# Chunked attention and two feed-forward layers on one core: a fourth attention tile in the banks of h, a fixed line of first loads, the sign of the weights moved from ScalarE to VectorE

## The chip, the cores and the metric

The kernel runs on one core of one Trainium2 chip. The metric is the device time of one execution in microseconds (us); several runs are timed and their median is taken. TensorE (PE) does matmuls and transposes, VectorE (DVE) and ScalarE (ACT) work element by element and read the matmul results out of PSUM, GpSimd (POOL) works on SBUF, and the queue of SyncE (SP) issues every DMA of this kernel. Each engine takes its instructions in the order of its queue.

## The reference, cut to what matters

```
# attention within chunks of 64 tokens; 4 batches, 8 heads, 576 tokens, head size 64
scores = scale * (q_c @ k_c.T);  scores -= scores.max(-1)
attn = exp(scores);  attn = attn / (attn.sum(-1) + 1e-09)
x = (attn @ v_c)                         # as 2304 tokens x 512
h = x @ w_in1;   g = max(h, 0) + log1p(exp(-abs(h)));   x = g @ w_out1
h = x @ w_in2;   g = P(h) / (Q(h) + 1e-6);              out = g @ w_out2
```

Inputs arrive as 8-byte floats; w_in is 512 x 2048 and w_out 2048 x 512 in both layers. P is a cubic and Q a quadratic in |h| with four and two given coefficients.

## The kernel before

**Tiling.** Attention works on 18 tiles of 128 tokens. The layers work on five blocks of tokens, BLOCKS (L25): 512, 512, 512, 384 and 384, in the order 0, 3, 4, 1, 2 (L26, L27). A block passes through 16 steps, one for each slice of 128 hidden units: a step is twelve matmuls into h (`products_h`, L750), the activation on ACT, DVE and POOL (`softplus`, L787, or `rational`, L812), and twelve matmuls (nine or twelve in layer 2) into acc. A product of two 4-byte floats is made of three matmuls: each operand is split into a rounded high part and a low part, the rest (`split`, L282). ACT or POOL writes the high part, DVE or POOL the low part.

**Weights.** A weight chunk is loaded as 8-byte words and put together in `prepare` and `complete`: ACT makes a magnitude out of the upper words (`magnitude`, L338), DVE shifts it (`shift`, L351) and ORs in three bits of the lower words (`merge`, L357). Where a chunk is signed, ACT keeps the sign with a Prelu, which needs the table set EXP_LN loaded; where it is not, the magnitude is a Copy, which asks for no set, and DVE merges the sign with a second `merge`. Then the chunk is split: the high part of w_in on ACT, that of w_out on POOL (L389), both low parts on DVE. SIGNED (L36) covers the sixteen steps of block 0, in which all chunks of layer 1 are converted, two to a step. The softplus of those steps needs ACT's other set, so `table` (L254) loads a set each time the two alternate.

**Start.** Block 0 needs attention tiles 0 to 3 (STARTING) before its first product, h_0. A tile is: transposes of q and k on PE (L512), taken to SBUF by ACT (L524, into `room` for the first four tiles), scores (L558), maximum, subtraction, exponential, total, guard, reciprocal and division (L576 to L611, ACT only for the exponential), a transpose of the result (`turn_e`, L618), taken by ACT (L640), times v (`values`, L647), and split into xT (L290 on ACT, L298 on DVE). The tiles need two PSUM banks each: tiles 0 and 3 take the pair of pool ps_att, one after the other, tiles 1 and 2 the two pairs of ps_acc. The two banks of ps_h hold h; the first is used ahead of that by `warm`, matmuls of an identity with itself (`keep_warm`, L1150) that fill the time in which the plan has PE idle before h_0. Tiles 12, 13 and 14 follow within block 0; the others are done beside blocks 3, 4 and 1, with q and k and the result turned on DVE.

**Order.** All work is put down as tasks with an engine, a cost in us and what they depend on (`Program.add`, L68). `schedule` (L168) lists them several times, backwards for due times and forwards, first by the earliest due time, and keeps the list that ends soonest by these costs; the instructions are then emitted in that order of time. So a change of one cost or one dependence can move instructions on every queue. `alloc` ties tasks that take buffers of one pool into the order in which the buffers turn.

Of the kernel before, what the change touches and what calls it, by code (L numbers as in the profile page):

```python
# [11 lines left out]
F32 = mybir.dt.float32  # L12
# [23 lines left out]
SIGNED = range(0, 16)  # L36
# [3 lines left out]
E_BY_VECTOR = {*range(4, 12), *range(15, 18)}  # L40


class Program:
# [49 lines left out]

    def run(self, links, counts, place, free, pick, place_of):
# [34 lines left out]
    def forward(self, place):  # L129
        loaded = [None]  # L130
# [59 lines left out]
def tile_chunk_attention_two_ffn(  # L190
# [91 lines left out]
    def split(dst, src, hi_eng, lo_eng, cost, reads, key, alloc=None, before=None):  # L282
# [20 lines left out]
        add(lo_eng, lo_cost, lo, [*reads, (key, 0)], [(key, 1)])  # L303
# [17 lines left out]
    def prepare(name, after, signed):  # L321
# [47 lines left out]
        add(DMA, 2.2, load, [], [rkey], alloc="raw", after=after)  # L369
# [5 lines left out]
    def complete(name, rkey, mkey, shift, merge, signed):  # L375
# [5 lines left out]
        if layer == 1 or fc in DIRECT:  # L381
            key = wkey[name] = turn("w" + which, FC)

            def alloc():
# [4 lines left out]
                lambda n: wts[name][:, n], lambda: x["m", name], ACT if which == "i" else POOL,  # L389
# [39 lines left out]

    xT = {}  # L430
# [4 lines left out]
    unfinished = []  # L435
# [8 lines left out]
    def attention(tb):  # L444
# [3 lines left out]
        by_chunk = tb in E_BY_VECTOR  # L448
        o0 = 4 * CH if by_chunk else 0
# [70 lines left out]
        def take(n):  # L520
            def f():
                if n == 0:
                    new_turned()
                act.activation(  # L524
                    tiles["qkT"][:, n].rearrange("p g t -> p (g t)"), ps[0][:, n], AF.Copy
# [20 lines left out]
        def scores():  # L546
# [3 lines left out]
            for g in range(4):  # L550
                for c in range(2):
                    for h in range(2):
                        part_h, chunk = slice(64 * h, 64 * h + 64), slice(c * CH, (c + 1) * CH)
                        o0 = (2 * g + c) * CH
                        o = ps[0][part_h, 0, o0 : o0 + CH]
# [13 lines left out]
        def sc():  # L569
            if by_chunk:  # L570
                return ps[0][:, :, : 4 * CH].rearrange("p h (g k) -> p h g k", k=CH)
            return ps[0][:, 0].rearrange("p (m k) -> p m k", k=CH)
# [37 lines left out]
        def divide():  # L610
            vec.tensor_tensor(  # L611
# [4 lines left out]
        def turn_e():  # L616
            for g in range(4):
                pe.transpose(  # L618
                    ps[0][:, 0, g * P : (g + 1) * P],
# [18 lines left out]
        def take_e():  # L638
            tiles["aT"] = new_e(1)
            act.activation(tiles["aT"].rearrange("p m k -> p (m k)"), ps[0][:, 0], AF.Copy)  # L640

        def values():
            for g in range(4):
                for c in range(2):
                    for h in range(2):
                        part_c = slice(c * CH, (c + 1) * CH)
                        pe.matmul(  # L647
                            ps[0][64 * h : 64 * h + 64, c, o0 + g * CH : o0 + (g + 1) * CH],
# [10 lines left out]
        def half(n):  # L659
            tile = xT[1, j][:, n, :, part * TB : (part + 1) * TB]  # L660
            return tile.rearrange("p g (c t) -> p g c t", c=2)

        def result():
# [38 lines left out]
        if not by_chunk:  # L702
            add(DMA, 1.46, load_v, [], [(vkey, 0)])
# [14 lines left out]
        add(DVE, 0.6, divide, [ke, ks], [ke])  # L718
# [478 lines left out]
```

## Time and profile before

| | |
|---|---|
| median of 3 runs | 859.34 us (859.08 to 859.9) |
| the profiled execution's own time | 860.32 us |
| its span, first to last instruction | 858.5 us |
| granted clock of TensorE, mean | 0.999 |
| busy: PE, DVE, ACT, POOL | 99%, 75%, 59%, 30% of the span |
| ACT_TABLE_LOAD | 35 of 1.283 us, 31 of them between 31.4 and 127.4 us |
| first matmul of h_0 | 31.46 us |
| first matmul of block 3 (end of block 0's steps) | 127.38 us |

The profile lists the instructions of one execution with start and duration. Busy time says how much of a stretch an engine worked; the chain of waits and the idle time before an instruction say what it waited for. The profiled execution lies 1.0 us above the median, and 1.8 us of its time lie outside its span.

### The profile page before, as it was taken

What the parts mean: (1) busy time and instruction counts of PE and PEld (TensorE: products, weight loads), DVE (VectorE), ACT (ScalarE), POOL (GpSimd) and SP (SyncE); (2) the same over time, 40 slices, a digit from 0 to 9 for tenths busy, and PEclk for the clock granted to TensorE, in tenths of its full rate; (3) what the DMA queues carried; (4) which work ended last, traced back from release to release, by engine and by line L of the source; (5) the groups of instructions that cost most, each with busy time, mean ns of one, the idle gap of its engine ahead of it and who ended that gap; (6) DMA issues with size and microseconds to landing.
All of it is one profiled execution on the core that took longest, in us unless ns stands there. A gap on an engine that the chain in (4) does not pass through costs nothing.

```text
span 858.5 us, 13274 instructions
## 1 busy us (share of the span) xinstructions
PE 846.5 (99%) x5070; PEld 729.4 (85%) x5070; DVE 646.6 (75%) x1102; ACT 505.7 (59%) x862; POOL 258.3 (30%) x238
## 2 busy tenths in 40 slices
PE   8999999999999999999999999999999999999997
PEld 8777889999999888888778888899889888888886
DVE  3877788798899987217956687878787787788684
ACT  4899983323335323344447675768667776667683
POOL 0132432122321222143363622342252162222121
PEclk9999999999999999999999999999999999999999
DMA  9874535112552443246532200100200020000001
GB/s 204 210 224 149 192 104 124 38 50 84 167 144 74 147 111 100 74 136 205 172 101 90 84 0 1 50 1 1 75 12 1 7 80 0 1 14 36 0 1 49
DMA packets 76927, 71.11 MB, mean 83 GB/s; under 512 B 36160, under 2 KB 63808, under 8 KB 76864
## 3 DMA queue, kind: packets, MB, share of 16 engines
q1 hardware_dynamic: 76864, 70.27, 28.4%
q8 instruction: 39, 0.64, 0.3%
q14 instruction: 24, 0.20, 0.1%
HBM read 56.63 MB, written 13.63 MB: 82 GB/s over the span
## 4 chain that ended last, share of the span: by engine, by line
PE 79%; DVE 13%; issue 3%; ACT 3%; DMA 1%; POOL 0%; SPq 0%; DVEq 0%; ACTq 0%; POOLq 0%
PE h L759 38%; PE acc L951 22%; PE acc L921 16%; DVE qkT L537 4%; DVE aT L631 2%; DVE cm_2o L362 1%; PE aps L558 1%; DVE cm_2i L362 1%; PE warm L1153 1%; DVE t L832 1%; PE aps L647 1%; DMA wr_2o<-in_moe_w_out_dram 1%; PE aps L512 1%; DVE sm L601 1%; DVE mx L576 0%
## 5 line engine op out<-in xcount | busy, mean ns | idle before, releaser
L921 PE MATMUL acc<-g,w_1o 128*128 128x512 f32 (+1 forms) x960 | 211.7, 369 | 0.0
L759 PE MATMUL h<-xT,w_1i 128*128 128x512 f32 (+1 forms) x960 | 210.2, 369 | 1.5 <-ACT g L799 1.3
L759 PE MATMUL h<-xT,w_2i 128*128 128x512 f32 (+1 forms) x960 | 209.3, 368 | 0.4 <-DVE t L832 0.4
L951 PE MATMUL acc<-w_2o,g 128*128 128x512 f32 x864 | 208.9, 391 | 0.6 <-DVE ev L986 0.5
L759 PEld LDWEIGHTS h<-xT,w_2i 128*128 128x128 f32 x960 | 175.8, 188 | 26.0 <-DVE t L832 1.4
L759 PEld LDWEIGHTS h<-xT,w_1i 128*128 128x128 f32 x960 | 174.1, 188 | 25.3 <-ACT g L799 2.7
L921 PEld LDWEIGHTS acc<-g,w_1o 128*128 128x128 f32 x960 | 174.1, 188 | 23.0 <-DVE ev L986 0.2
L951 PEld LDWEIGHTS acc<-w_2o,g 128*128 128x128 f32 x864 | 161.3, 188 | 34.8 <-POOL g L862 1.8
L862 POOL TENSOR_TENSOR g<-t,g 128x512 fp32r<-128x512 f32 (+1 forms) x80 | 94.6, 1182 | 263.1 <-ACT g L859 221.9
L802 POOL TENSOR_TENSOR g<-t,g 128x512 fp32r<-128x512 f32 (+1 forms) x80 | 99.9, 1248 | 223.3 <-ACT g L799 209.6
L794 ACT ACTIVATE t<-h 128x512 f32<-128x512 f32 (+1 forms) x80 | 44.2, 552 | 93.8 <-PE h L759 93.7
L799 ACT ACTIVATE g<-h 128x512 fp32r<-128x512 f32 (+1 forms) x80 | 44.3, 554 | 65.4 <-PE acc L921 59.9
L537 DVE STREAM_TRANSPOSE qkT<-qk 32x256 f32<-32x256 f32 x176 | 76.8, 437 | 5.7 <-PE aps L558 2.4
L832 DVE SCALAR_TENSOR_TENSOR t<-u,absb_t,t 128x512 f32<-128x512 f32 (+1 forms) x80 | 55.4, 694 | 30.5 <-ACT u L829 17.4
L888 DVE TENSOR_TENSOR t<-h,t 128x512 f32<-128x512 f32 (+1 forms) x80 | 50.8, 635 | 34.6 <-ACT t L847 21.0
L851 ACT ACTIVATE u<-t,epsq_t 128x512 f32<-128x512 f32 (+1 forms) x80 | 52.0, 650 | 37.5 <-DVE t L832 35.5
L832 DVE SCALAR_TENSOR_TENSOR t<-t,epsq_t,u 128x512 f32<-128x512 f32 (+1 forms) x80 | 55.4, 692 | 20.5 <-ACT u L855 20.1
L859 ACT ACTIVATE g<-t 128x512 fp32r<-128x512 f32 (+1 forms) x80 | 46.8, 586 | 37.0 <-DVE t L832 36.7
L832 DVE SCALAR_TENSOR_TENSOR t<-t,na_t,h 128x512 f32<-128x512 f32 (+1 forms) x80 | 55.4, 693 | 10.9 <-ACT t L847 7.0
L847 ACT ACTIVATE t<-h,b_t 128x512 f32<-128x512 f32 (+1 forms) x80 | 51.0, 640 | 18.0 <-PE h L759 10.4
L877 ACT ACTIVATE t<-h,na_t 128x512 f32<-128x512 f32 (+1 forms) x80 | 58.4, 730 | 4.5 <-PE h L759 4.5
L832 DVE SCALAR_TENSOR_TENSOR u<-t,na_t,u 128x512 f32<-128x512 f32 (+1 forms) x80 | 55.7, 697 | 0.0
(79 smaller groups left out, 751.6 us busy)
## 6 DMA issues: line engine op xcount, KB each, us to landing
wr_1i<-in_moe_w_in_dram SPq DMA_DIRECT2D x16, 512.0 KB, 3.8
wr_1o<-in_moe_w_out_dram SPq DMA_DIRECT2D x16, 512.0 KB, 4.5
wr_2i<-in_moe_w_in_dram SPq DMA_DIRECT2D x16, 512.0 KB, 4.0
wr_2o<-in_moe_w_out_dram SPq DMA_DIRECT2D x16, 512.0 KB, 3.8
out_dram<-ev SPq DMA_DIRECT2D x18, 256.0 KB, 2.1
qk<-in_q_dram SPq DMA_DIRECT2D x16, 256.0 KB, 5.3
qk<-in_k_dram SPq DMA_DIRECT2D x16, 256.0 KB, 5.9
v<-in_v_dram SPq DMA_DIRECT2D x16, 256.0 KB, 4.6
```

The lines of the kernel that those rows point to most:

```text
L537: vec.transpose(tiles["qkT"][p0 : p0 + 32, n, :, c * CH : (c + 1) * CH].rearrange("p g (u t) -> p g t u", t=2), qk_t[tb][p1 : p1 + 32, h:: ...
L759: pe.matmul(hs[s], w[:, a, c * P : (c + 1) * P], xt[:, b, c, :n_tok], start=n == 0, stop=n == 3 * KC - 1,)
L802: pool.tensor_tensor(out=gs[s][:, 1, :n_tok], in0=t["t2"], in1=gs[s][:, 0, :n_tok].bitcast(F32), op=ALU.subtract,)
L832: return lambda: vec.scalar_tensor_tensor(out=out(), in0=in0(), scalar=scalar, in1=in1(), op0=op0, op1=op1)
L847: act.activation(new("t1"), h(), AF.Abs, scale=b_t[:, 0:1])
L851: act.activation(u(), d(), AF.Ln, bias=epsq_t)
L859: act.activation(gs[s][:, 0, :n_tok], p(), AF.Copy)
L862: pool.tensor_tensor(out=gs[s][:, 1, :n_tok], in0=p(), in1=gs[s][:, 0, :n_tok].bitcast(F32), op=ALU.subtract,)
L877: lambda: act.activation(new("t2"), h(), AF.Identity, scale=na_t[:, 3:4], bias=na_t[:, 2:3]),
L888: lambda: vec.tensor_tensor(out=p(), in0=h(), in1=p(), op=ALU.mult), [hkey, kp], [kp],
L921: pe.matmul(accs[1, j, half][:, c % 2, :n_tok], wts[1, "o", fc][:, a, c * P : (c + 1) * P], gs[s][:, b, :n_tok], start=first and n == 0, s ...
L951: pe.matmul(accs[2, j, half][:, c % 2], gs[s][:, b, c * P : (c + 1) * P], wts[2, "o", fc][:, a, :], start=first and n == 0, stop=last and ...
```

## The change

Five things are changed.

1. **Tile 3 in the banks of h** (`apart`): the fourth tile takes the two banks of ps_h as two tiles of one bank each, instead of the pair of ps_att after tile 0. Its result is split bank by bank, in two halves on ACT and on DVE. `warm` gives its bank up when tile 3 takes its own, and from then on nothing fills PE's idle time until tile 0's low part of xT is done; after that `warm_2` takes the pair of ps_att.
2. **First loads in a fixed line** (`in_line`, FIRST_LOADS): sixteen loads are tied in the order q and k of the four tiles, v of tiles 0 and 1, w_in chunk 0, v of 2 and 3, w_in chunk 1, w_out chunk 0, q of tile 12. A second line puts tile 12's transposes behind tile 3's result.
3. **Sign of the weights**: SIGNED is now range(2), so the chunks put down in steps 0 and 1 (w_in 0 to 2, w_out 0 and 1) stay as they were, and of the other 27 chunks DVE merges the sign with an instruction of its own. The magnitudes of these no longer ask for EXP_LN.
4. **Rounding**: ACT, not POOL, writes the high part of the w_out chunks of layer 1 that are not signed.
5. **Costs in the plan**: loads of q, k and v 1.2 us (were 1.45 and 1.46), of weights 1.5 us (were 2.2), and the plan starts with EXP_LN loaded. DIVIDE_BY_POOL is empty and so does nothing.

```
-SIGNED = range(0, 16)
+SIGNED = range(2)
+FIRST_LOADS = "q0 k0 q1 k1 q2 k2 q3 k3 v0 v1 i0 v2 v3 i1 o0 q12".split()
...
+    def in_line(self, tasks):
+        for a, b in zip(tasks, tasks[1:]):
+            self.deps[b].setdefault(a, 0.0)
...
-        add(DMA, 2.2, load, [], [rkey], alloc="raw", after=after)
+        loads[which, fc, layer] = add(DMA, 1.5, load, [], [rkey], alloc="raw", after=after)
...
-                lambda n: wts[name][:, n], lambda: x["m", name], ACT if which == "i" else POOL,
+                lambda n: wts[name][:, n], lambda: x["m", name], ACT if which == "i" or (layer == 1 and not signed) else POOL,
...
+        apart = tb == STARTING[-1]
...
+        def bank(n):
+            return ps[n] if apart else ps[0][:, n]
+
         def new_ps():
+            if tb not in STARTING[:-1]:
+                x["warm"] = None
+            if apart:
+                for n in range(2):
+                    ps[n] = ps_h.tile([P, 512], F32, tag="h", name=f"aps_{tb}_{n}")
+                return
...
+        def result(c=None):
+            if apart:
+                return ps[c][:, : 4 * CH].rearrange("p (g t) -> p g t", t=CH)
...
+        if apart:
+            alloc = "h"
...
-        b0, b1 = (slot, 0), (slot, 1)
+        b0, b1 = (turn("h", 2), turn("h", 2)) if apart else ((slot, 0), (slot, 1))
...
-            split(half, result, ACT, DVE, 512, [b0, b1], (xkey[1, j], part), "x", new_x)
+            if not apart:
+                done[tb] = split(
+                    half, result, ACT, DVE, 512, [b0, b1], (xkey[1, j], part), "x", new_x
+                )
+                return
+            for c, b in ((0, b0), (1, b1)):
+                done[tb] = split(
+                    lambda n, c=c: half(n, c), lambda c=c: result(c), ACT, DVE, 256, [b],
+                    (xkey[1, j], (part, c)), "x", new_x,
+                )
...
+    prog.in_line(
+        [loads[(l[0], int(l[1:]), 1) if l[0] in "io" else (l[0], int(l[1:]))] for l in FIRST_LOADS]
+    )
+    prog.in_line([done[STARTING[-1]], begin[STAGED[len(STARTING)], 0]])
...
-            for _ in range(int(time / 0.22)):
+            for _ in range(int(time / 0.22) if x["warm"] else 0):
                 pe.matmul(x["warm"][:, :P], ident, ident, start=True, stop=True)
...
+            if i == done[STARTING[0]]:
+                x["warm"] = ps_att.tile([P, 2, 512], F32, tag="att", name="warm_2")[:, 0]
```

In the rows that follow, names end in a running number of the buffer. qk_117 to qk_120 hold q and k of tiles 0 to 3, qk_121 those of tile 12, v_141 to v_144 v of tiles 0 to 3; room_0 and room_1 are a tile's buffers, with room_0_133 and room_1_134 those of tile 0 and two numbers more for each next tile.

SP's queue before, from its fourth load to its seventeenth:

```order
L467 DMA qk_119<-in_q_dram 128x8x64
L467 DMA qk_118<-in_q_dram 128x8x64
...
L467 DMA qk_120<-in_k_dram 128x8x64
L486 DMA v_143<-in_v_dram 128x8x64
L486 DMA v_144<-in_v_dram 128x8x64
L486 DMA v_142<-in_v_dram 128x8x64
L467 DMA qk_121<-in_q_dram 128x8x64
L329 DMA wr_1i_344<-in_moe_w_in_dram 128x4x256
L329 DMA wr_1i_375<-in_moe_w_in_dram 128x4x256
L334 DMA wr_1o_390<-in_moe_w_out_dram 128x1024
L467 DMA qk_121<-in_k_dram 128x8x64
```

and SP's queue now, from its eighth load to its seventeenth:

```order
L480 DMA qk_120<-in_k_dram 128x8x64
L499 DMA v_141<-in_v_dram 128x8x64
L499 DMA v_142<-in_v_dram 128x8x64
L340 DMA wr_1i_270<-in_moe_w_in_dram 128x4x256
L499 DMA v_143<-in_v_dram 128x8x64
L499 DMA v_144<-in_v_dram 128x8x64
L340 DMA wr_1i_332<-in_moe_w_in_dram 128x4x256
L345 DMA wr_1o_344<-in_moe_w_out_dram 128x1024
L480 DMA qk_121<-in_q_dram 128x8x64
L480 DMA qk_121<-in_k_dram 128x8x64
```

The same seventeen transfers stand there. The last q and k of the four tiles moved from ninth to eighth place, w_in chunk 0 from fourteenth to eleventh, w_out chunk 0 from sixteenth to fifteenth; k of tile 12 stays seventeenth.

PE's queue before, from tile 2's scores to h_0 (aps_306 is the pair of ps_att in tile 3's hands, aps_161 the same pair in tile 0's, aps_459 in tile 12's):

```order
L558 MATMUL aps_215<-room_0_137 64x64 x16
L512 MATMUL aps_306<-ident,qk_120 128x128 x8
L1153 MATMUL warm<-ident 128x128 x3
L558 MATMUL aps_306<-room_0_139 64x64 x16
...
L618 MATMUL aps_306<-ident,room_1_140 128x128 x4
L1153 MATMUL warm<-ident 128x128 x4
L647 MATMUL aps_306<-room_1_140,v_144 64x64 x16
L1153 MATMUL warm<-ident 128x128 x6
L512 MATMUL aps_459<-ident,qk_121 128x128 x8
L1153 MATMUL warm<-ident 128x128 x3
L759 MATMUL h_0_481<-xT_280,w_1i_124 128x512 x12
```

and now (aps_0_244 and aps_1_245 are the two banks of h in tile 3's hands):

```order
L580 MATMUL aps_209<-room_0_137 64x64 x16
L534 MATMUL aps_1_245<-ident,qk_120 128x128 x4
L641 MATMUL aps_161<-ident,room_1_134 128x128 x4
L580 MATMUL aps_0_244<-room_0_139 64x64 x16
L670 MATMUL aps_161<-room_1_134,v_141 64x64 x16
...
L1199 MATMUL warm_381<-ident 128x128
L641 MATMUL aps_0_244<-ident,room_1_140 128x128 x4
...
L1199 MATMUL warm_381<-ident 128x128 x10
L534 MATMUL aps_451<-ident,qk_121 128x128 x8
L798 MATMUL h_0_468<-xT_330,w_1i_124 128x512 x12
```

Tile 3's scores moved ahead of tile 0's values; before, they stood behind the end of tile 0. The matmuls of `warm` between them are gone, and ten stand together ahead of tile 12's transposes.

ACT's queue before, from the softplus of step 0 to that of step 2 (cm is a magnitude, t and g are the softplus, once whole and once rounded):

```order
L258 ACT_TABLE_LOAD
L347 ACTIVATE cm_1i_542<-wr_1i_445 128x512
L347 ACTIVATE cm_1o_545<-wr_1o_465 128x512
L597 ACTIVATE e_540<-e_540 128x512
L258 ACT_TABLE_LOAD
L799 ACTIVATE g_563<-h_1_521 128x512
L794 ACTIVATE t_1_578<-h_1_521 128x512
L290 ACTIVATE w_1i_126<-cm_1i_542 128x512
L258 ACT_TABLE_LOAD
```

and now, the steps after that:

```order
L360 ACTIVATE cm_1i_620<-wr_1i_530 128x512
L360 ACTIVATE cm_1o_622<-wr_1o_547 128x512
L301 ACTIVATE w_1o_642<-cm_1o_545 128x512
L301 ACTIVATE xT_651<-aps_451 128x4x128
L301 ACTIVATE w_1i_128<-cm_1i_620 128x512
L840 ACTIVATE g_683<-h_3_658 128x512
```

The table loads are gone from the steps (35 in the whole queue before, 5 now), and the high part of w_out came to ACT. On DVE a second merge, L373, follows each first one from chunk w_in 3 on.

## Rows read from the trace of the kernel before

**Rows 1.** The page: busy us, share of the span, instructions.

```profile
PE 846.5 (99%) x5070; PEld 729.4 (85%) x5070; DVE 646.6 (75%) x1102; ACT 505.7 (59%) x862; POOL 258.3 (30%) x238
```

**Rows 2.** Busy times by stretch: length, engines' busy us, granted clock, DMA share, GB/s.

```profile
0.00:31.40 31.40, 27.97 (x401) 25.54 (x402) 16.67 (x35) 15.33 (x26) 0.70 (x6) 1.00 0.94 206
...
31.40:63.40 32.00, 31.38 (x227) 24.94 (x227) 25.41 (x41) 30.30 (x42) 10.17 (x10) 1.00 0.81 214
```

**Rows 3.** Who PE waited for, 31.4 to 127.4: us, times, longest.

```profile
PE aps L558 <- ACT qkT L524: 0.6, 2, 0.3
PE aps L618 <- DVE e L611: 0.3, 1, 0.3
```

**Rows 4.** The chain that ended last: start, us, what (one of many).

```profile
89.47 2.72 PE h L759 x12
```

**Rows 5.** Timeline of the start: start, us, engine, line, what, idle before.

```profile
9.74 0.69 DVE L576 TENSOR_REDUCE mx<-aps 128x8 f32<-128x512 f32 x1 [8.84 <-PE aps L558]
...
13.19 0.60 ACT L524 ACTIVATE room<-aps 128x512 f32<-128x512 f32 x1 [0.26 <-PE aps L512]
...
20.59 1.15 PE L558 MATMUL aps<-room 64*64 64x64 f32 x32 [0.51 <-ACT room L524]
...
25.58 0.69 DVE L611 TENSOR_TENSOR room<-room,sm 128x512 f32<-128x512 f32 x1
...
29.20 0.69 DVE L298 TENSOR_TENSOR xT<-aps,xT 128x512 fp32r<-128x512 f32 x1 [1.08 <-ACT xT L290]
...
29.94 1.09 PE L512 MATMUL aps<-ident,qk 128*128 128x128 f32 x8
...
31.46 3.01 PE L759 MATMUL h<-xT,w_1i 128*128 128x512 f32 x12
```

**Rows 6.** The same timeline, neighbours on DVE.

```profile
23.96 0.68 DVE L601 TENSOR_REDUCE sm<-room 128x8 f32<-128x512 f32 x1
...
24.55 0.68 DVE L298 TENSOR_TENSOR xT<-aps,xT 128x512 fp32r<-128x512 f32 x1
...
25.15 0.16 DVE L605 TENSOR_SCALAR sm<-sm 128x8 f32<-128x8 f32 x1
```

**Rows 7.** DMAs: issue on SP, us from issue to landing (last number), one-us stretch.

```profile
17.45 0.50 SPq L334 DMA_DIRECT2D wr_1o<-in_moe_w_out_dram  x1
18.00 0.75 SPq L467 DMA_DIRECT2D qk<-in_k_dram  x1
...
wr_1o<-in_moe_w_out_dram SPq DMA_DIRECT2D x1, 512.0 KB, 8.4
qk<-in_k_dram SPq DMA_DIRECT2D x1, 256.0 KB, 8.7
...
11.00:12.00 1.00, 1.00 (x12) 1.00 (x11) 0.30 (x2) 0.79 (x2) 0.00 (x0) 1.00 1.38 217
```

**Rows 8.** Groups of one shape, 31.4 to 127.4: busy us, mean ns, idle before.

```profile
L298 DVE TENSOR_TENSOR w_1o<-cm_1o,w_1o 128x512 fp32r<-128x512 f32 x15 | 17.9, 1194 | 2.0 <-POOL w_1o L292 2.0
L298 DVE TENSOR_TENSOR w_1i<-cm_1i,w_1i 128x512 fp32r<-128x512 f32 x16 | 14.6, 910 | 10.2 <-ACT w_1i L290 9.9
L362 DVE SCALAR_TENSOR_TENSOR cm_1o<-wr_1o,cm_1o 128x512 uint32<-128x512 uint32 x16 | 11.0, 685 | 0.0
...
L353 DVE TENSOR_SCALAR cm_1o<-cm_1o 128x512 uint32<-128x512 uint32 x15 | 6.4, 425 | 1.3
...
L258 ACT ACT_TABLE_LOAD x31 | 39.8, 1283 | 0.6
L347 ACT ACTIVATE cm_1o<-wr_1o 128x512 f32<-128x512 f32 x15 | 9.9, 663 | 0.1
...
L802 POOL TENSOR_TENSOR g<-t,g 128x512 fp32r<-128x512 f32 x15 | 20.8, 1386 | 20.5 <-ACT g L799 8.7 <-issue 5.5 <-ACT t L794 4.2
```

**Rows 9.** The same timeline: weight loads of `warm` matmuls, early and later.

```profile
1.35 3.49 PEld L1153 LDWEIGHTS warm<-ident 128*128 128x128 f32 x16 [1.35 <-POOL ident masks.py:199]
...
9.54 1.64 PEld L1153 LDWEIGHTS warm<-ident 128*128 128x128 f32 x14
```

More of the change, by code (lines that the diff above doesn't have):

```diff
@@ L302, in split @@
         add(hi_eng, hi_cost, hi, reads, [(key, 0)], alloc=alloc)
-        add(lo_eng, lo_cost, lo, [*reads, (key, 0)], [(key, 1)])
+        return add(lo_eng, lo_cost, lo, [*reads, (key, 0)], [(key, 1)])
     def convert(layer, chunks, after=(), signed=False):
@@ L428, in runs @@
             done += step
+    loads = {}
     xT = {}
@@ L524, in f @@
                 act.activation(
-                    tiles["qkT"][:, n].rearrange("p g t -> p (g t)"), ps[0][:, n], AF.Copy
+                    tiles["qkT"][:, n].rearrange("p g t -> p (g t)"), bank(n), AF.Copy
                 )
@@ L554, in scores @@
                         o0 = (2 * g + c) * CH
-                        o = ps[0][part_h, 0, o0 : o0 + CH]
+                        o = bank(0)[part_h, o0 : o0 + CH]
                         if by_chunk:
@@ L571, in sc @@
                 return ps[0][:, :, : 4 * CH].rearrange("p h (g k) -> p h g k", k=CH)
-            return ps[0][:, 0].rearrange("p (m k) -> p m k", k=CH)
+            return bank(0).rearrange("p (m k) -> p m k", k=CH)
         def maximum():
@@ L618, in turn_e @@
                 pe.transpose(
-                    ps[0][:, 0, g * P : (g + 1) * P],
+                    bank(0)[:, g * P : (g + 1) * P],
                     tiles["e"][:, 2 * g : 2 * g + 2].rearrange("p c k -> p (c k)"),
@@ L639, in take_e @@
             tiles["aT"] = new_e(1)
-            act.activation(tiles["aT"].rearrange("p m k -> p (m k)"), ps[0][:, 0], AF.Copy)
+            act.activation(tiles["aT"].rearrange("p m k -> p (m k)"), bank(0), AF.Copy)
         def values():
@@ L657, in new_x, with half @@
                 xT[1, j] = xpool.tile([P, 2, KC, T], F32R, tag="xT", name=f"xT_{j}")
-        def half(n):
+        def half(n, c=slice(0, 2)):
             tile = xT[1, j][:, n, :, part * TB : (part + 1) * TB]
-            return tile.rearrange("p g (c t) -> p g c t", c=2)
-        def result():
+            return tile.rearrange("p g (c t) -> p g c t", c=2)[:, :, c]
+        def result(c=None):
+            if apart:
+                return ps[c][:, : 4 * CH].rearrange("p (g t) -> p g t", t=CH)
             return ps[0][:, :, o0 : o0 + 4 * CH].rearrange("p c (g t) -> p g c t", t=CH)
@@ L678, in attention @@
         for n in range(2):
-            add(
-                DMA, 1.45, load_qk(n), [],
+            loads["qk"[n], tb] = add(
+                DMA, 1.2, load_qk(n), [],
                 [(qkey, n)] if n else [qkey, (qkey, 0), (qkey, 1)],
@@ L702, in attention @@
         if not by_chunk:
-            add(DMA, 1.46, load_v, [], [(vkey, 0)])
+            loads["v", tb] = add(DMA, 1.2, load_v, [], [(vkey, 0)])
             add(
@@ L717, in attention @@
         add(DVE, 0.16, invert, [ks], [ks])
-        add(DVE, 0.6, divide, [ke, ks], [ke])
+        if tb in DIVIDE_BY_POOL:
+            add(POOL, 1.3, divide, [ke, ks], [ke])
+        else:
+            add(DVE, 0.6, divide, [ke, ks], [ke])
         if tb in E_BY_VECTOR:
@@ L765, in products_h @@
         parts = range(n_tok // TB) if layer == 1 else range(KC)
+        if layer == 1 and STARTING[-1] in tiles_of(j):
+            parts = [*parts[:-1], (parts[-1], 0), (parts[-1], 1)]
         reads = [(wk, 0), (wk, 1)] + [((xkey[layer, j], c), n) for c in parts for n in range(2)]
```

16 lines of the change are left out of this document (9 added, 7 removed).

## The prediction

> **What bounds the kernel now.** I read the busy shares first: PE is busy for 99% of the span [rows 1]. Then the stretches: up to 31.4 us PE's time goes to attention and to `warm` matmuls that compute nothing, and DVE works only 16.67 us of it; from 31.4 us on PE is busy for 31.38 of 32 us [rows 2]. A group of twelve matmuls of 512 columns goes by in 2.72 us [rows 4], and groups follow each other almost without a gap: the waits of PE in block 0 sum to 0.9 us, 0.6 of them on ACT [rows 3]. So behind the first product the time is PE's own work, and that work isn't changed. What can be won is the moment at which h_0 begins, 31.46 us [rows 5], and the few waits; what can be lost is that some engine no longer feeds PE. ACT was the nearest to that in block 0, busy for 30.30 of 32 us [rows 2], because 31 table loads took 39.8 us there [rows 8].
>
> The sums stand against the profiled execution, 860.32 us with a span of 858.5. Its own time is 0.98 above the median of 859.34; I carry differences over to the median.
>
> **The start.** Three queues end at h_0, and I cost each.
>
> *DVE.* Tile 0's q and k stay first and second, so its maximum still starts at 9.74. Tile 1's k now lands fourth and not sixth, so PE can go on with it at once: four transposes (half of the 1.09 for eight), ACT's take 0.60, scores 1.15 [rows 5], 0.1 for hand-overs, so tile 1's maximum starts at 12.1. From there to the last thing that h_0's bank waits for (the low part out of tile 3's first bank) DVE's queue holds 33 instructions: 20 of full width, 4 pairs of guard and reciprocal, 3 shifts, 2 halves. Full ones follow each other every 0.60 (23.96, 24.55, 25.15 [rows 6]), a pair takes 25.58 - 25.15 = 0.43 [rows 5, 6], a shift 0.42 [rows 8], a half some 0.36 (estimate from half of 0.69). 12.0 + 1.72 + 1.27 + 0.72 = 15.7, so 27.8 if DVE never waits. That is a floor.
>
> *Tile 3.* Before, its scores stood at 20.59, behind tile 0's hold on the pair of ps_att, and its division at 25.58; h_0 came 5.88 after that division [rows 5]. Now its scores need no bank of tile 0. Its division has 22 of the 33 before it (13 full, 4 pairs, 1 shift: 9.9), so it starts at 22.0, and 22.0 + 5.88 = 27.9. The one `warm` that now takes tile 0's pair stands ahead of tile 3's second transposes and waits for tile 0's low part, which is next on DVE: 0.6 more, 28.5.
>
> *Loads.* ACT's queue has the magnitudes of w_in 1 and w_out 0 ahead of the last three high parts of xT and of w_in 0's rounding; so h_0 waits for the landing of w_out 0. Before, that was 17.45 + 8.4 = 25.85 [rows 7]. It moves from sixteenth to fifteenth, past one load of 256 KB, which at 217 GB/s takes 1.2 us [rows 7]: 24.65. Then ACT: magnitude 0.66 [rows 8], 0.60, two halves of 0.36, 0.60 [rows 5]; DVE: 0.69 and 0.36; 0.2 for hand-overs: 28.5. If it lands no sooner than before, 29.7. Tile 12's k stays seventeenth, lands at 18.00 + 8.7 = 26.7 [rows 7], and its transposes (1.09) allow h_0 at 27.8.
>
> I take 28.5, where two of the three meet, bounds 27.8 and 29.7: 31.46 - 28.5 = 2.96 us won, at least 1.8, at most 3.7.
>
> **The clock, an item without a row of its own.** `warm` filled PE's gaps up to 31.4; PE was busy for 27.97 us and the granted clock stood at 1.00 [rows 2]. Now nothing fills them from tile 3's first transposes (some 12 us) to 23 us, and PE works about half of that time in pieces of about one us. The first `warm` weight loads took 3.49 / 16 = 0.218 us each, those at 9.54 1.64 / 14 = 0.117 [rows 9]: the lower level, 1.2 GHz, was at work early though the column says 1.00, and after some five us of work the engine ran at 2.4. I cost the gaps at nothing, because by the sums above PE has some work in every two us, and keep the price below. The Trainium skill, TensorE: Matmul & The Clock Gate, Part 1, says that an idle engine is put back to half its clock and gets it back by work. By that rule the gaps are a risk and not a certainty, since PE is not wholly idle; what it would cost is the second rival, and no run here shows it yet.
>
> **Block 0, ACT.** 30 of the 35 table loads go. Per step ACT loses some two times 1.283 and gains one rounding of about 0.6 for w_out. Two of the three waits in block 0 are on ACT (0.6 in all [rows 3]): I count them as gone. The bound is 0 to 0.9.
>
> **Block 0, DVE.** 27 more merges at 0.685 [rows 8] are 18.5 us, at the spacing of 0.60 16.2. DVE was busy 25.41 of 32 us [rows 2]; ten merges more in such a stretch, at 0.60, make 31.4. That would be full, but part of the 25.41 was waiting: w_out's low parts took 1194 ns on average and w_in's 910 where such an instruction takes 0.69 [rows 5, 8], 0.5 and 0.2 us longer. By spacings a step needs two shifts, four merges and two low parts: 0.84 + 2.4 + 1.2 = 4.4 us, with 0.7 for the delays 5.1, against 5.44 us of PE (two groups of 2.72 [rows 4]). An attention tile adds some 3.6 us on DVE and some 2.8 on PE. Eight steps with nearly three tiles: 8 x 5.1 + 10.8 = 51.6 against 8 x 5.44 + 8.4 = 51.9. It just fits, and weights are converted two or three steps ahead; so I cost the merges at nothing, with PE's matmuls as the cover. Without that cover it is the first rival. What speaks against me in the Trainium skill is SBUF — State Buffer, "Who interferes with whom": a DVE instruction with two SBUF inputs and a GpSimd instruction that reads SBUF shut each other out for a whole instruction. The merges have two such inputs, yet their mean is 685 ns with no delay in it, while the low parts show it [rows 8]; by the rule twice as many merges beside POOL's 1386 ns would sooner meet it, and the sum would go to the first rival.
>
> **POOL, splitting tile 3, the rest.** POOL loses 14 roundings; it was far from full, and nothing waited long for it (2.0 us of DVE [rows 8]), so nothing is won but fewer collisions. The two halves of tile 3's split cost one more instruction on ACT and on DVE; they are in the sums. From block 3 on the work is the same in another order, since the plan's costs moved. Of PE's 12.0 us of idle time [rows 1] 3.4 lie before 31.4 and 0.6 in the next 32 us [rows 2], so 8 are left, the tail among them. I take 0, with one us either way.
>
> **Sum.** 860.32 - 2.96 - 0.6 = 856.8 for the profiled execution, 859.34 - 3.56 = 855.8 for the median. With the bounds (1.8 to 3.7, 0 to 0.9): 854.7 to 857.5.
>
> **Rivals.** *First, slower: DVE becomes the bound of block 0.* Place: conversions, from w_in 3 on. With the durations instead of the spacings, and with the delays that the low parts show now, a step costs 0.85 + 4 x 0.685 + 0.91 + 1.19 = 5.69 us [rows 8], 0.25 above PE's 5.44; fourteen steps lose 3.5, and three tiles at about 1.0 each 3.0. 855.8 + 6.5 = 862.3. It decides from the point at which both low parts together take more than 5.44 - 3.59 = 1.85 us. For it: 2.10 now. Against it: instructions of DVE overlap by 0.09, and POOL now has one instruction a step. Chance 0.10.
>
> *Second: the clock falls in the start.* Then tile 3's last transposes and values (some 1.1 us), ten `warm` (twenty loads of 0.117, 2.3 [rows 9]) and tile 12's transposes (1.09 [rows 5]) take twice as long, 4.5 us more. h_0 would start at 33 instead of 28.5, though by then the work has brought the clock back: 855.8 + 4.5 = 860.3. For it: a half-empty PE from 12 to 23 us; against it: pieces of work in every us or two. Chance 0.13.
>
> *Third: the start doesn't move as it should*, because the loads land no sooner or the old waits return through `warm` and the queue of ACT: h_0 at 30.5 to 31, 0.7 won, 858.6. Chance 0.10.
>
> *Fourth: the new order also closes later waits*, a good us more with h_0 at 27.8: 853.9. Chance 0.10.
>
> **How the numbers follow.** The forecast, 855.8, has 0.57. A difference of 0.2% is 1.7 us, about what a measurement of this kernel can tell from none, so faster means under 857.6 and slower above 861.1. Faster: the forecast but for 0.02, the fourth rival, a little of the second and third, 0.68. Same: the second and third and that rest, 0.22. Slower: the first, 0.10. The range reaches from 853.6 (the fourth) to 860.4 (the second) and leaves out the first rival and the ends.
>
> **What would show it.** Right: h_0 between 27.8 and 29.7; tile 3's scores by 17; DVE without gaps from 12 to 28; five table loads; the same 2.72 per group behind h_0; no new row of PE waiting in block 0. Wrong: granted clock below 1 or transposes of twice the length between 15 and 30; PE waiting for low parts of w_1i or w_1o on DVE; merges well above 685 ns; w_out 0 landing at 26 or later.

## The result: 10.7 us slower, and the profile after

| | before | after |
|---|---|---|
| median, same chip | 859.57 us | 870.24 us (869.68 to 870.96) |
| ratio | | 1.0123, 95% interval 1.0111 to 1.0135 |
| the profiled execution, its span | 860.32, 858.5 | 870.76, 868.6 |
| first matmul of h_0 | 31.46 us | 30.36 us |
| ACT_TABLE_LOAD | 35 | 5 |

The forecast was 855.8 us. PE's work is what it was, so the loss must show as idle time or as slow time of PE. The page of the changed kernel: busy us, share of the span, instructions; then the granted clock of PE in 40 slices of 21.7 us.

```profile
PE 848.0 (98%) x5026; PEld 729.5 (84%) x5026; DVE 653.8 (75%) x1130; ACT 476.2 (55%) x847; POOL 250.9 (29%) x224
...
PEclk9899999999999999999998999999999999999999
```

Against [rows 1] PE is busy for about the same time (848.0 and 846.5 us) in a span that is 10 us longer. The clock falls in two slices, the second (the start) and the twenty-second (near 470 us). Busy times by stretch of the changed kernel, against [rows 2]: length, busy us of PE, PEld, DVE, ACT, POOL, granted clock, DMA share, GB/s.

```profile
0.00:31.40 31.40, 26.44 (x363) 23.32 (x364) 17.69 (x39) 16.14 (x29) 1.32 (x7) 0.89 1.07 235
31.40:63.40 32.00, 32.00 (x229) 25.87 (x228) 28.09 (x49) 20.76 (x37) 8.32 (x6) 1.00 0.78 198
63.40:95.40 32.00, 32.00 (x233) 25.80 (x232) 29.86 (x50) 19.77 (x37) 8.01 (x5) 1.00 0.55 165
```

Block 0 is now perfect: PE 32.00 of 32 us, and the list of its waits from 31.4 to 127.4, which answers to [rows 3], is empty. ACT fell from 30.30 to 20.76 us, DVE rose to 28 and 30 (30.11 in the stretch from 95.4 to 127.4, where PE has 32.00 again). So neither the merges nor the roundings lost the time. The longest rows of PE's waits over the whole span (us in total, times, longest) name the place:

```profile
PE h L798 <- DVE t L873: 4.0, 3, 1.9
PE acc L992 <- DVE ev L1027: 3.8, 2, 2.9
PE h L798 <- ACT g L840: 2.6, 2, 2.4
```

All three lie behind 131 us, in work that no line of the diff touches. PE's timeline shows the four longest there (start, us, line, what, in brackets the idle time before and who ended it):

```profile
435.24 3.02 PE L798 MATMUL h<-xT,w_1i 128*128 128x512 f32 x12 [2.36 <-ACT g L840]
...
468.84 5.49 PE L992 MATMUL acc<-w_2o,g 128*128 128x512 f32 x12 [2.86 <-DVE ev L1027]
...
634.19 2.37 PE L798 MATMUL h<-xT,w_2i 128*128 128x384 f32 x12 [1.11 <-DVE t L873]
...
774.54 4.61 PE L798 MATMUL h<-xT,w_2i 128*128 128x512 f32 x12 [1.92 <-DVE t L873]
```

Behind 131 us the waits of PE sum to 10.4 us, in the kernel before to 2.2. And some cost twice: the twelve matmuls at 468.84 took 5.49 us and those at 774.54 4.61, where a group takes about 3. The stretches behind 468.84 show why, in the column before the last two:

```profile
468.00:470.00 2.00, 1.16 (x3) 0.96 (x4) 1.82 (x4) 1.97 (x4) 1.28 (x1) 0.52 0.20 80
470.00:472.00 2.00, 2.00 (x7) 1.52 (x6) 1.42 (x3) 1.17 (x3) 0.00 (x0) 0.50 0.45 182
...
474.00:476.00 2.00, 2.00 (x8) 1.55 (x8) 1.72 (x4) 1.62 (x3) 2.00 (x3) 0.77 0.83 247
```

After the wait the granted clock is 0.50, the lower of the two levels, 1.2 GHz, for some five us in which PE works; from 476 on it is 1.00 again. The Trainium skill, TensorE: Matmul & The Clock Gate, Part 1, says that the throttled state is the default and work releases it; these rows agree.

The account of the profiled executions: h_0 1.1 us earlier, block 0's waits 0.5 less, later waits 8.2 more, slow matmuls some 4.5 (2.6 at 468.84, 1.6 at 774.54, the rest beside them): 11.1 where 10.4 was measured.

### The profile page after: what moved, and what is told of

Same layout as the page of the kernel before. It is cut to its first block, busy times and chain, and to the rows that moved or that the text cites. A ratio compares the mean times of both kernels' runs of the same rounds, so it can differ in the third digit from the quotient of the medians.

```text
span 868.6 us, 13181 instructions
## 1 busy us (share of the span) xinstructions
PE 848.0 (98%) x5026; PEld 729.5 (84%) x5026; DVE 653.8 (75%) x1130; ACT 476.2 (55%) x847; POOL 250.9 (29%) x224
## 4 chain that ended last, share of the span: by engine, by line
PE 76%; DVE 13%; ACT 6%; issue 4%; POOL 1%; DMA 0%; DVEq 0%; POOLq 0%; ACTq 0%
PE h L798 35%; PE acc L992 19%; PE acc L962 18%; DVE t L873 4%; DVE qkT L559 2%; DVE t L929 1%; ACT t L918 1%; ACT t L888 1%; PE aps L580 1%; PE aps L670 1%; PE warm L1199 1%; ACT u L870 1%; ACT u L892 1%; DVE cm_2i L373 1%; DVE cm_2o L373 1%
## 5 line engine op out<-in xcount | busy, mean ns | idle before, releaser
L798 PE MATMUL h<-xT,w_2i 128*128 128x512 f32 (+1 forms) x960 | 211.8, 371 | 4.0 <-DVE t L873 4.0
L992 PE MATMUL acc<-w_2o,g 128*128 128x512 f32 x864 | 211.1, 394 | 3.8 <-DVE ev L1027 3.8
L870 ACT ACTIVATE u<-h 128x512 f32<-128x512 f32 (+1 forms) x80 | 43.4, 542 | 24.0 <-PE h L798 13.1
```

The lines of the kernel that those rows point to most:

```text
L798: pe.matmul(hs[s], w[:, a, c * P : (c + 1) * P], xt[:, b, c, :n_tok], start=n == 0, stop=n == 3 * KC - 1,)
L870: act.activation(u(), h(), AF.Square)
L992: pe.matmul(accs[2, j, half][:, c % 2], gs[s][:, b, c * P : (c + 1) * P], wts[2, "o", fc][:, a, :], start=first and n == 0, stop=last and ...
```

## The experiments

A list is the order that the planner gives to all tasks of a kernel. In seven of the twelve kernels that follow this list is replaced by a fixed one (`pinned` in the diffs), in six of them joined from two lists: the tasks that a kernel's own plan puts before 125 us (131 in one) in its own order, which is the start and block 0, and the rest in the order of a second kernel.

### Which part of the span: change two orders crosswise

**The changed kernel with the late order of before.**

```
-        for i, t in prog.schedule():
+        for i, t in pinned():      # own list up to 125 us, then that of before
```

> The changed kernel, with its own order up to the end of block 0 (the first 125 us of the plan) and the order of the kernel before from there on. Theory A (the loss of 10.7 us lies in the order that the planner gives to the rest, with waits of PE at 435.24 (2.36 us), 468.84 (2.86), 634.19 (1.11) and 774.54 (1.92) in the changed kernel and half the clock behind two of them): h_0 at 30.4 as in the changed kernel, the four waits gone, the clock full from 30 us on, and a time of 857.5 to 858.5, which is 859.6 less the 1.1 us of h_0 and up to 0.9 of block 0's waits. Theory B (the changed parts themselves cost: DVE's second merges, ACT's roundings, half the clock in the start): about 870, the same as the changed kernel, with the waits moved elsewhere.

858.13 us, ratio 0.9977 (0.9968 to 0.9987), h_0 at 30.24. With the late order of before the change wins 1.5 us; the four long waits are gone and those of the kernel before are back (0.83 and 0.51 for ACT g, 0.55 for DVE ev, 0.44 for DVE t).

**The kernel before with the late order of the changed one.** The same edit the other way round.

```
-        for i, t in prog.schedule():
+        for i, t in pinned():      # own list up to 125 us, then that of the changed kernel
```

> The kernel before, with its own order for the first 125 us of the plan and the order of the changed kernel from there on. None of the five parts of the change is in it; only the order behind block 0. Theory A (order): waits of PE of 2 to 3 us before the first acc of layer 2 and near 435, 635 and 775 us, and a time of 869 to 872, as slow as the changed kernel or 1 to 2 us slower. Theory B (the parts themselves): 859 to 860, like the kernel before.

872.71 us, ratio 1.0143 (1.012 to 1.0167). No part of the change is in this kernel, and its PE timeline repeats the rows above, 2.6 to 3.5 us later:

```profile
437.84 4.43 PE L858 MATMUL h<-xT,w_1i 128*128 128x512 f32 x12 [2.35 <-ACT g L898]
...
472.34 5.49 PE L1050 MATMUL acc<-w_2o,g 128*128 128x512 f32 x12 [2.85 <-DVE ev L1085]
...
778.02 4.61 PE L858 MATMUL h<-xT,w_2i 128*128 128x512 f32 x12 [1.92 <-DVE t L931]
```

Theory A holds both ways: the loss is the order of the rest. Here the wait of 2.35 us lowers the clock as well, which the one at 435.24 didn't (4.43 us for twelve matmuls against 3.02).

### One wait: four instructions moved

**The changed kernel in its own order, with the two ACT and two DVE copies of layer 1's last acc ahead of the next rational step.** In the changed kernel PE had done that acc at 463.3 us, and ACT's and DVE's copies stood here:

```profile
463.99 0.76 ACT L918 ACTIVATE t<-h,na_t 128x512 f32<-128x512 f32 x1
...
466.17 0.58 ACT L870 ACTIVATE u<-h 128x512 f32<-128x512 f32 x1 [0.83 <-DVE t L929]
466.66 1.08 ACT L1025 ACTIVATE ev<-acc 128x512 f32<-128x512 f32 x2
...
468.11 1.28 DVE L1027 COPY ev<-acc 128x512 f32<-128x512 f32 x2
```

They stand behind a chain in which ACT and DVE wait for each other (0.83 us here), so the copies are late though nothing that they need is.

```
-..., t (ACT), t (ACT), u (ACT), ev, ev (ACT), ..., t (DVE), t (DVE), t (DVE), ev, ev (DVE)
+..., ev, ev (ACT), t (ACT), t (ACT), u (ACT), ..., ev, ev (DVE), t (DVE), t (DVE), t (DVE)
```

> The changed kernel in its own order, but for four instructions: the two ACT and two DVE copies that empty layer 1's last acc stand at the head of what is queued when that acc is done, and not behind the t and u of the next rational step. Theory A1 (each wait is the place of a few instructions in one queue, and half the clock behind it doubles it): the wait of 2.86 us at 468.84 goes, the twelve matmuls behind it take 2.9 and not 5.49 us, the other waits stay: 870.2 - 5.4 = 864.8, 864 to 866. Rival B1 (the step is bound by the ACT and DVE chain of rational, so the copies only push the wait to the next h): 869 to 871, with a new wait for DVE t of 2 us or more behind it.

865.21 us, ratio 1.0064 (1.0047 to 1.0081): 5.0 us less than the changed kernel. ACT, DVE and PE there now:

```profile
463.36 1.07 ACT L1126 ACTIVATE ev<-acc 128x512 f32<-128x512 f32 x2
...
464.10 1.28 DVE L1128 COPY ev<-acc 128x512 f32<-128x512 f32 x2
...
465.20 2.88 PE L1093 MATMUL acc<-w_2o,g 128*128 128x512 f32 x12
...
474.03 3.01 PE L899 MATMUL h<-xT,w_2i 128*128 128x512 f32 x12 [0.38 <-DVE t L974]
```

No wait here, twelve matmuls in 2.88 and not 5.49 us, and 0.38 us of it back at a later h. In the traces the lead over the changed kernel grows from 0.6 us (462.48 against 463.11 for the last h ahead of it; h_0 came at 29.77 in this execution, which the edit doesn't touch) to 5.8 (628.37 against 634.19): 5.2 us for the four instructions, where A1 had 5.4. Behind that two things cancel, so the other waits did not just stay:

```profile
768.66 3.04 PE L899 MATMUL h<-xT,w_2i 128*128 128x512 f32 x12 [1.92 <-DVE t L974]
...
781.29 1.66 PE L1093 MATMUL acc<-w_2o,g 128*128 128x512 f32 x6 [1.43 <-DVE ev L1128]
```

The wait of 774.54 is there again, but without slow matmuls behind it, and a wait of 1.43 us is new. That a wait of this kind is the place of a few instructions is shown for this one; the other waits were not moved.

### Is it the change, or the draw of a list?

**Another seed of the planner's shaken due times, in the changed kernel (3, 4) and in the kernel before (3); the plan's load costs of the change alone in the kernel before; the old load costs in the changed kernel.**

```
-    SEED, SHAKEN = 2, 3
+    SEED, SHAKEN = 3, 3
...
-        add(DMA, 2.2, load, [], [rkey], alloc="raw", after=after)
+        add(DMA, 1.5, load, [], [rkey], alloc="raw", after=after)
```

> The changed kernel with another seed of the planner's shaken due times, nothing else. Theory A2 (the loss is the luck of one list): other waits at other places and a time anywhere from 857 to 872, most likely not 870. Rival H (the change makes every list bad, since the plan now counts loads at 1.2 and 1.5 us and so expects an end of 842 us where it expected 854): 867 to 873 again, with the wait at the change of layers.

> The kernel before with another seed of the planner's shaken due times, nothing else. Theory A3 (the rest of the span is a lottery of lists, and the list of before was a good draw): 861 to 868, with waits of 1 to 3 us behind 130 us. Theory H3 (the lists of before are good and those of the changed kernel bad, for a reason in the change): 859 to 860.5, no wait above 1 us.

> The changed kernel with a third seed, nothing else. Theory A3: other waits again, anywhere from 857 to 872. Theory H3: 864 to 872, as with the two other seeds (870.2 and 864.9).

> The kernel before with only the plan's costs of the change: loads at 1.2 and 1.5 us, the plan begun with the first table set loaded. No instruction is added or taken away. Theory K (the cheaper loads alone let the planner pack the lists too tight, and that is the loss): 865 to 872 with waits of 2 us and more at the change of layers. Theory A3 (any change of the tasks draws another list): between 858 and 868.

> The changed kernel with the plan's costs of loads as before (2.2, 1.45 and 1.46 us). Theory K: the loss goes, 857 to 860, no wait above 1 us behind 130 us. Theory A3: it stays in part, 860 to 868, with other waits.

| list | median us | ratio (95%) | h_0 | PE's waits, 31 to 131 | 131 to the end |
|---|---|---|---|---|---|
| before | 859.44 to 859.75 | 1 | 31.46 | 0.9 | 2.2 |
| before, seed 3 | 862.22 | 1.0031 (1.0017 to 1.0046) | 30.30 | 2.0 | 4.0 |
| before, new costs | 864.22 | 1.0062 (1.0044 to 1.0081) | 33.39 | 0.2 | 3.4 |
| changed | 870.24 | 1.0123 (1.0111 to 1.0135) | 30.36 | 0.4 | 10.4 |
| changed, seed 3 | 864.89 | 1.0051 (1.0035 to 1.0068) | 26.89 | 2.4 | 6.8 |
| changed, seed 4 | 864.20 | 1.0055 (1.0025 to 1.0085) | 27.83 | 2.2 | 6.2 |
| changed, old costs | 877.84 | 1.0218 (1.0174 to 1.0262) | 28.50 | 5.0 | 11.9 |

Theory K falls: with the old costs the changed kernel got slower, and the new costs in the kernel before gave no wait above 1.62 us. A3 stands only in part. It had 860 to 868 for the old costs and "other waits"; but five waits of the changed kernel come again there in the same order and length, 7.8 to 9.1 us later, two of them these:

```profile
477.91 4.60 PE L992 MATMUL acc<-w_2o,g 128*128 128x512 f32 x12 [2.85 <-DVE ev L1027]
...
782.35 4.61 PE L798 MATMUL h<-xT,w_2i 128*128 128x512 f32 x12 [1.91 <-DVE t L873]
```

Likewise the kernel before keeps its waits of 0.55 us (552.31, with the new costs 555.77) and 0.43 (628.38, 631.81). So these costs left the waits of the rest mostly as they were, and they are not what drew the changed kernel's order. It is the seeds that brought other waits at other places (1.97 us for ACT ev at 692.32 with seed 3, 2.64 for POOL g at 439.09 with seed 4). The seven lists are therefore some five draws; they lie between 859 and 878 us, and that of before is the best of its three. The three of before lie at 859 to 864, the four of the changed kernel at 864 to 878: whether the change itself makes worse lists likelier, as theory H3 has it, so few draws don't tell (seed 4's 864.20 lies in the ranges of A3 and H3 both), and this stays open, as does which part of the change drew the new order. Of the 3.1 us by which the profiled execution with the new costs is longer than that of the kernel before (863.39 and 860.32), h_0 (1.9) and the waits (0.5) explain 2.4; the rest is open.

### The parts of the change, with the late order held

**Sign and rounding alone** (late order of before).

```
-SIGNED = range(0, 16)
+SIGNED = range(2)
...
-                lambda n: wts[name][:, n], lambda: x["m", name], ACT if which == "i" else POOL,
+                lambda n: wts[name][:, n], lambda: x["m", name], ACT if which == "i" or (layer == 1 and not signed) else POOL,
```

> The kernel before with only the sign merged on DVE and the rounding of w_out on ACT, its start as before, and the order behind block 0 that of the kernel before. Theory A (DVE has room for 27 merges, ACT's two waits of 0.6 us go): 858.7 to 859.6, 5 table loads or a few more, no wait of PE in block 0 above 0.5 us. Theory B (DVE bounds block 0, the first rival of the prediction): 862 to 866, with rows of PE waiting on DVE low parts between 40 and 127 us.

860.35 us, ratio 1.0006 (0.9997 to 1.0016): no difference, and no wait of PE for DVE's low parts above 0.2 us in block 0. Theory B, the first rival, is out. But theory A missed as well, by 0.75 us: PE waited 0.75 us for a tile's division on DVE and 0.57 for ACT's rounding of w_in, where A had nothing above 0.5. And the start is not quite that of before: in this kernel's own list h_0 comes at 30.39, 1.1 us earlier, of which nothing is left (the h that starts at 628.38 in the kernel before starts at 628.49).

**The start alone** (the changed kernel, weights as before, late order of before).

```
-SIGNED = range(2)
+SIGNED = range(0, 16)
```

> The changed start alone (tile 3 in the banks of h, the line of first loads, the plan's costs), the weights signed and rounded as in the kernel before with their 31 table loads, own order for the first 125 us of the plan and the order of before from there on. Theory A: h_0 at 30.4 with half the clock from 21 to 27 us, about 1 us less than before: 858.3 to 858.8; the sign change then adds 0 to 0.5 us of gain at most in block 0. Rival G (without the sign change ACT has no room for an earlier start and takes it back in block 0): 859.3 to 860.5 with PE waiting for ACT between 31 and 127 us.

859.51 us, ratio 0.9997 (0.9988 to 1.0006), though h_0 began at 26.87, 4.6 us earlier. Most of the gain is gone by 125 us, in three waits of PE that sum to 4.6 us (at 425 us the lead over the kernel before is 1.1: 425.10 against 426.23):

```profile
38.04 0.65 PE L742 MATMUL aps<-ident,e 128*128 128x128 f32 x4 [1.42 <-DVE e L735]
...
59.55 0.66 PE L742 MATMUL aps<-ident,e 128*128 128x128 f32 x4 [1.41 <-DVE e L735]
...
124.37 2.56 PE L1063 MATMUL acc<-g,w_1o 128*128 128x512 f32 x10 [1.79 <-DVE w_1o L410]
```

DVE, on which PE waited, itself waited for ACT between 30 and 125 us (us, times, longest), where the crosswise run with both halves of the change has 5.2 and 1.3 for the same two (cm_1i, w_1i):

```profile
DVE cm_1i L465 <- ACT cm_1i L459: 7.6, 5, 1.8
DVE w_1i L410 <- ACT w_1i L402: 6.3, 8, 1.0
```

Rival G reads this as ACT having no room for an earlier start beside its table loads. The time fits its range, but the trace doesn't show that cause. The kernel before has about as much of the two waits (2.9 and 9.9) with 0.9 us of waits of PE; ACT is busy for 27.57, 29.91 and 24.34 us of the three stretches of 32 us here, and for 30.30, 30.40 and 30.17 there. Nor do late loads hold it: no row has ACT waiting for a DMA. Ahead of each of PE's three waits DVE works without a gap. Ahead of the first two there stands an instruction far longer than others of its kind (0.69 and 0.68 us); ahead of the third stand ten transposes of q and k of other tiles, from 118.19 to 123.59, and only behind them the low part for which PE waited, though its high part was written at 117.88:

```profile
34.44 1.78 DVE L410 TENSOR_TENSOR w_1o<-cm_1o,w_1o 128x512 fp32r<-128x512 f32 x1
...
53.83 1.81 DVE L474 SCALAR_TENSOR_TENSOR cm_1o<-wr_1o,cm_1o 128x512 uint32<-128x512 uint32 x1
...
123.62 0.69 DVE L410 TENSOR_TENSOR w_1o<-cm_1o,w_1o 128x512 fp32r<-128x512 f32 x1
```

So the gain went in DVE's queue; how much of that the table loads are to blame for stays open. Neither half of the change wins anything alone; together they win 1.5 us with h_0 only at 30.24.

### What held h_0 at 30.3

**The first of the crosswise pair, with PE's gaps filled.**

```
+            if apart:                    # behind tile 3's scores
+                x["warm"] = ps[1]
...
+                if apart:                # behind tile 3's values
+                    x["warm"] = ps_att.tile([P, 2, 512], F32, tag="att", name="warm_2")[:, 0]
...
-            if i == done[STARTING[0]]:
-                x["warm"] = ps_att.tile([P, 2, 512], F32, tag="att", name="warm_2")[:, 0]
```

> As the first of these four, but with the gaps of PE between tile 3's scores and its values filled: the warm matmuls write into tile 3's second bank, which is free between the copy of k and the values, and warm_2 takes the pair of ps_att only behind tile 3's values. Theory C (half the clock is what puts h_0 at 30.36 and not at the 28.5 forecast): the granted clock stays at 1.00 from 16 to 30 us, turn_e takes 0.66 and not 1.12, and h_0 starts at 29.2 to 29.4, where DVE's last low part of xT (29.09 in the changed kernel) becomes the end: 1.0 us less than the first of the four, so 856.5 to 857.5. Rival D (the clock costs nothing there because DVE ends last anyway): h_0 at 30 or later and no difference, under 0.3 us.

In the changed kernel PE's timeline of the start, to be set beside [rows 5], reads:

```profile
18.97 0.66 PE L641 MATMUL aps<-ident,room 128*128 128x128 f32 x4 [1.65 <-DVE room L634]
...
21.20 1.12 PE L641 MATMUL aps<-ident,room 128*128 128x128 f32 x4 [0.19 <-DVE room L634]
22.74 0.80 PE L1199 MATMUL warm<-ident 128*128 128x128 f32 x2 [0.42 <-DVE xT L309]
23.33 1.06 PE L641 MATMUL aps<-ident,room 128*128 128x128 f32 x4
24.32 1.99 PE L670 MATMUL aps<-room,v 64*64 64x64 f32 x64
26.24 3.22 PE L1199 MATMUL warm<-ident 128*128 128x128 f32 x20
...
30.36 2.99 PE L798 MATMUL h<-xT,w_1i 128*128 128x512 f32 x12
```

From 21.20 on four transposes take 1.1 us and not 0.66, and the `warm` matmuls, put there to fill idle time, take 3.22 us and stand ahead of tile 12's transposes and h_0. Three of the changed kernel's stretches, and then the last of them and the twenty rows of `warm` in this one:

```profile
16.00:18.00 2.00, 1.32 (x62) 1.18 (x58) 2.00 (x6) 1.52 (x4) 0.00 (x0) 1.00 1.13 189
18.00:20.00 2.00, 0.66 (x4) 0.42 (x4) 2.00 (x4) 1.41 (x3) 0.00 (x0) 1.00 0.88 253
...
22.00:24.00 2.00, 1.58 (x8) 1.25 (x6) 1.88 (x4) 0.60 (x1) 0.00 (x0) 0.50 1.30 244
```

```profile
22.00:24.00 2.00, 1.94 (x69) 1.56 (x69) 1.85 (x4) 1.47 (x3) 0.00 (x0) 1.00 1.05 292
...
23.91 2.50 PE L1304 MATMUL warm<-ident 128*128 128x128 f32 x20
```

The clock stays at 1.00 and h_0 comes at 27.32, 2.9 us earlier than in the pair's first and more than theory C hoped: DVE's last part had itself been waiting for slow transposes. By the rows at both levels the same matmuls of PE take some 2.5 us less (our estimate: 0.5 and 0.4 for the transposes, 0.5 for the values, 1.1 for `warm`); the other 0.4 is the wait for tile 0's low part at 22.74, which the edit takes away too.

This price hangs on what stands in PE's queue. In the kernels with the start alone and with seeds 3 and 4 the clock falls as well (to 0.60 and 0.54 from 20 to 24 us in the first), and h_0 comes at 26.87, 26.89 and 27.83. No `warm` stands between the second transposes of tiles 2 and 3 there, and ten or twelve rows of it, not twenty, stand ahead of tile 12's:

```profile
20.94 1.97 PE L742 MATMUL aps<-ident,room 128*128 128x128 f32 x8
...
24.36 1.60 PE L1300 MATMUL warm<-ident 128*128 128x128 f32 x12
...
26.87 3.00 PE L899 MATMUL h<-xT,w_1i 128*128 128x512 f32 x12
```

So the slow clock and the `warm` matmuls put in against it held h_0 together.

The median is 857.61, ratio 0.9975 (0.9964 to 0.9987), 0.5 us less than the pair's first, which the two intervals don't tell apart: neither C nor D, under which h_0 would not have moved. The profiled execution shows where the rest went:

```profile
37.42 0.66 ACT L461 ACTIVATE cm_1o<-wr_1o 128x512 f32<-128x512 f32 x1 [3.09 <-DMA wr_1o<-in_moe_w_out_dram]
...
43.09 1.11 PE L744 MATMUL aps<-ident,e 128*128 128x128 f32 x4 [3.31 <-DVE e L737]
```

ACT waited 3.09 us for the load of w_out 2, DVE for ACT, and PE 3.31 us for DVE. This execution took 861.22 us, the slowest of its ten (the next took 858.47), so how long the wait is in the others isn't shown.

**The same, with the loads of tiles 13 to 15 behind more weight chunks**, two to six of them (the expectation says one to three, which holds for tile 13 alone). SP's queue from w_in 3 on, in the names of the chunks:

```
-i3, q13, o2, k13, i4, o3, v13, q14, k14, i5, v14, o4, v15
+i3, o2, i4, o3, q13, k13, i5, o4, v13, i6, o5, q14, k14, i7, o6, v14, i8, o7, v15
```

> As the run with tile 3's gaps filled and the late order of before, and with the loads of tiles 13, 14 and 15 moved behind one to three more weight chunks in SP's queue (w_out 2, w_in 4 and w_out 3 go ahead of tile 13's q and k). Theory E (h_0 came 3 us earlier there, at 27.3, but the weights of the next steps did not: the magnitude of w_out 2 waited 3.09 us for its DMA at 37.42 and PE 3.31 us at 43.09): the loads are what takes the gain back, w_out 2 lands 1.5 to 3 us earlier, the wait shrinks below 1 us, and the time is 855.5 to 856.5. Rival F (DVE, 4.00 of 4 us busy from 40 to 44, is the bound there whatever lands when): 857.3 to 858.

855.37 us (854.99 to 855.67), ratio 0.9946 (0.9932 to 0.9961): faster than both kernels, by 4.2 us and 15. Its magnitude of w_out 2 starts at 33.72 us, h_0 at 27.23, and PE's waits behind h_0 up to 131 us are 0.29 and, where the two lists join, 0.86 for ACT (127.28), which the pair's first has too. Theory E holds and F is out (857.3 to 858): h_0 is 3.0 us earlier than in the pair's first, and once the weights of the next steps come earlier too, the median is 2.8 less.

## Why the prediction was wrong, step by step

- **"From block 3 on the work is the same in another order ... I take 0, with one us either way."** This is the step that failed, and it carries most of the miss: the new order of the rest costs 13 us in the kernel before (872.71 against 859.6) and 12 of the 14.4 us of the miss in the changed kernel (870.24 against 858.13, forecast 855.8). The last 2.3 us lie ahead of it, in the start above all. I took "PE is at 99%" as a property of the work; it was one of a good list. PE's few waits behind 131 us [rows 1, 2] were read as the most that could go; of the seven lists they are the least (2.2 us, the others 3.4 to 11.9). The reason given, "since the plan's costs moved", doesn't hold for the costs of the loads, with which these waits stayed.
- **"I cost the gaps at nothing."** Wrong by 2.9 us of h_0 (30.24 against 27.32), by our estimate some 2.5 of them the clock and 0.4 the wait for tile 0's low part. PE worked 1.32 of the two us from 16 to 18, and 0.66 from 18 to 20, and the clock was at 0.50 from 22 on. The second rival named this mechanism, but alone put 4.5 us on it.
- **The sums of the start** came near where the clock held, h_0 at 27.3 against a forecast of 28.5, but not every term was right, so part of that is luck. The floor of 27.8 was none: DVE's last low part of xT did end there (27.73 and 27.62 in the two kernels with the gaps filled), but h_0's first matmul began ahead of that end (27.32 and 27.23). In the changed kernel tile 3's division came at 21.39 (forecast 22.0). The term for the loads was too long: w_out 0 landed at 22.3 (17.32 and 5.0), not at 24.65.
- **Block 0, ACT**: right. Five table loads, the waits gone.
- **Block 0, DVE**: right, the first rival was not met. 28.09 us of 32 where I had 31.4 (29.86 and 30.11 in the next two stretches). The low parts got shorter where the rounding is on ACT; against [rows 8], 31.4 to 127.4 now,

```profile
L373 DVE SCALAR_TENSOR_TENSOR cm_1i<-wr_1i,cm_1i 128x512 uint32<-128x512 uint32 x27 | 19.5, 722 | 0.0
L373 DVE SCALAR_TENSOR_TENSOR cm_1o<-wr_1o,cm_1o 128x512 uint32<-128x512 uint32 x28 | 19.0, 680 | 0.1
L309 DVE TENSOR_TENSOR w_1i<-cm_1i,w_1i 128x512 fp32r<-128x512 f32 x14 | 12.9, 920 | 1.6 <-ACT w_1i L301 1.3
L309 DVE TENSOR_TENSOR w_1o<-cm_1o,w_1o 128x512 fp32r<-128x512 f32 x15 | 12.7, 847 | 1.0 <-ACT w_1o L301 1.0
```

w_out's low parts took 847 ns and not 1194 (1124 with the start alone, 731 with sign and rounding alone), the merges 680 and 722 with the second merges among them.
- **"2.96 us won" at h_0 is won at the end.** Wrong too, and seen only in the experiments: the start alone gave 4.6 us at h_0 and nothing at the end that a measurement tells (ratio 0.9997). My sum let PE's matmuls cover everything behind h_0, but the cover moves with h_0, while what feeds it doesn't: the load of w_out 2 in the kernel with the gaps filled, DVE's queue in that with the start alone.
- **Rivals.** None held the result. Three were of the start and of block 0; the fourth did name the later waits, but only as something that a new order could close (853.9). That it could open them, as the description of the order ahead of the prediction lets expect, had no rival.

## What to carry to other kernels

Where a planner or scheduler sets the order, an edit of one stage draws a new order for all of them: put a price on that from several draws (other seeds brought other waits here, other load costs mostly the same ones), and measure an edit with the rest of the list pinned. When PE is at 99%, look for what its few waits would be in another list, and try to move the few instructions that a long wait stands behind. An earlier start was won here only when what feeds the next steps, the loads above all, came earlier as well.

## What the runs showed of the hardware

- A wait of PE can cost twice, and its length alone doesn't decide it. In the changed kernel 2.36 us at 435.24 left the clock at 1.00, and behind 1.92 us at 774.54 it was 0.82 and 0.50; in the kernel before with the late order of the changed one it was 0.50 behind 2.35 us at 437.84. With the copies moved, the same wait of 1.92 us, for the same instruction and now at 768.66, left it at 1.00:

```profile
770.00:772.00 2.00, 2.00 (x11) 1.62 (x10) 1.27 (x2) 1.73 (x3) 0.00 (x0) 1.00 0.00 0
```

  What decides is left open.
- The granted clock of the changed kernel fell to 0.50 by 22 us without a long wait: the longest before that is 1.65 us, at 18.97, and PE was busy for 1.32 and 0.66 us of the two stretches of two us from 16 to 20.
